# One level of Strassen's algorithm in the second MLP's first product, for the last twelve token tiles of an attention and two-MLP kernel

## The chip, the cores and the metric

The kernel runs on one core of a Trainium2 chip. The core has five engines with a queue of instructions each: PE (TensorE) multiplies matrices, DVE (VectorE), ACT (ScalarE) and POOL (GpSimd) work on elements, and SP (SyncE) issues most of the DMAs. Instructions on one engine run in the order in which they stand; an instruction that waits holds up all behind it on that engine. PE reads from SBUF and writes into PSUM, which has eight banks of 512 columns. A weight load (PEld in the profile) puts a 128x128 block into the array, and a matmul then streams up to 512 columns past it.

The metric is the time of one execution on the device in microseconds (us), as the median of several runs.

## The reference

Four batches of eight heads with 576 positions and head size 64 go through causal attention with a bias; the result, 2304 tokens of 512 values, goes through two MLPs. The change lies in the second one:

```python
def _moe2_ref(x, w_in, w_out):          # x: 2304 x 512, w_in: 512 x 2048, w_out: 2048 x 512
    h = x @ w_in
    relu6 = np.clip(h + 3.0, 0.0, 6.0)
    g = h * relu6 / 6.0
    return (g @ w_out).astype(np.float32)
```

The weights come as float64 and have to keep more than one float32r word of precision. So every operand of a product is held as two float32r parts, a high and a low one, and every product is three passes: high by high, low by high, high by low.

## The kernel before

The kernel is written as a list of steps. `plan.add` (lines 56 to 92) takes an engine, an estimated duration, a function that issues the instructions, and what the step reads and writes. `Plan.emit` (lines 94 to 165) plays the list through with these estimates: each engine takes, among the steps that are ready, the one that was added first; a step that opens a PSUM bank waits until one of the eight is free. The order so found on each engine is the program. At run time engines wait for each other by semaphores, and the order on an engine is fixed.

The second MLP (from line 1009 on) works on 18 token tiles of 128, in five chunks of 3, 3, 4, 4 and 4 tiles (`CHUNKS`). The hidden size 2048 is cut into 16 blocks `m` of 128.

- `load_w2(m)` loads one block of both weights as float64 words, decodes it and splits it into high and low (`split64`: two ACT, three DVE and one POOL or DVE step for each 128x512 tile).
- `load_x2(ci)` loads a chunk's input, which the first MLP left transposed in DRAM (`x2_d`), and splits it.
- `ffn2_h(ci, m)` is the first product: four blocks of the 512 inputs by three passes are 12 matmuls of the chunk's width (384 or 512 columns) into one bank (line 1075). Then four steps make the second product's operand: ACT takes relu(h + 3) out of the bank (L1079), DVE takes the minimum with 6 and multiplies by h (L1083), ACT rounds that to its high part (L1087), DVE subtracts to get the low part (L1091).
- `ffn2_out(ci, m, t)` is the second product: for each token tile, three matmuls of 512 columns (line 1106) add onto a bank that the tile keeps until block 15. Then ACT moves it out (L1111) and SP stores it.

Chunks 0 and 1 run interleaved, so that they share the arriving weights; their six tiles hold six banks, and two banks are left for the first products. Chunks 2, 3 and 4 run one after the other, each with four banks held and four free. The second products of a block stand two blocks (`LAG = 2`) behind its first product:

```python
    for ci, m in items:
        ...
        ffn2_h(ci, m)
        ...
        late.append((ci, m))
        if len(late) > LAG:
            outs(*late.pop(0))
```

Of the kernel before, what the change touches and what calls it, by code (L numbers as in the profile page):

```python
# [188 lines left out]
def kernel(ctx, tc, q, k, v, s, w_in, w_out, g_ln, w2_in, w2_out, out):  # L189
# [820 lines left out]
    chunks = []  # L1010
    t0 = 0
    for n in CHUNKS:
        chunks.append((t0, n))
        t0 += n
    pools, w2, xc, g_t, ob_t = {}, {}, {}, {}, {}
# [12 lines left out]
    def load_w2(m):
        def part(x, i):
            if m not in w2:  # L1030
                w2[m] = pools["w2a" if m < EARLY else "w2b"].tile([P, 2, 2, 512], F32R, name=f"w2_{m}")
# [165 lines left out]
```

## Time and profile before

| | us |
|---|---|
| median of 3 runs (lowest, highest) | 840.14 (839.83, 841.47) |
| the profiled execution | 840.16 |
| its span, first to last instruction | 838.4 |
| chunks 0 and 1 interleaved, PE only on the second MLP | about 444 to 573 |
| chunks 2, 3 and 4 | 573.2 to 834.3 |

Stages do not overlap on PE after 444 us: what PE does from there is the second MLP alone. Busy times count from an instruction's start to its modelled end, and matmuls are pipelined, so that the next one starts before the last one's end; how long a matmul holds PE is read from the distance between two starts. The granted clock is 0.995 of full speed over the span and 1.00 in every stretch of the second MLP but the last.

### The profile page before, as it was taken

The page shows a single profiled execution, that of the slowest core. Times are in us where ns is not written, and L with a number is a line of the kernel's source. Part 1 is how long each engine was busy: PE and PEld are TensorE (multiplying, and loading weights), DVE is VectorE, ACT ScalarE, POOL GpSimd, SP SyncE. Part 2 cuts the span into 40 slices and gives each one's busy share as a digit, 9 for nine tenths or more (in the row PEclk, how much of TensorE's full clock was granted, in tenths as well). Part 3 has the DMA queues.
Part 4 walks back from the last instruction along what each step waited for, and adds up shares of the span by engine and source line. Part 5 has one row for each costly group of instructions (what it writes and reads, how often), then busy time and mean ns, then how long its engine had stood idle before and what let it go on. Part 6 is the DMA issues. An engine that isn't in the chain of part 4 may idle for free.

```text
span 838.4 us, 13540 instructions
## 1 busy us (share of the span) xinstructions
PE 811.5 (97%) x4864; PEld 686.6 (82%) x4864; DVE 437.7 (52%) x1126; ACT 399.1 (48%) x928; POOL 208.2 (25%) x308
## 2 busy tenths in 40 slices
PE   3899999999999999999999999999999999999998
PEld 2555588898898889888999999998888888888886
DVE  3677887746846675739826992233222232222221
ACT  2575767755765565736635762244222322232222
POOL 1563654424632354326412220000000000000000
PEclk9999999999999999999999999999999999999999
DMA  6753596756546455223615640012000300010001
GB/s 156 198 153 109 119 225 142 173 121 134 129 112 141 102 129 121 65 93 118 199 38 191 217 151 1 0 63 89 1 0 1 101 1 0 1 51 1 0 1 50
DMA packets 95938, 77.52 MB, mean 92 GB/s; under 512 B 64288, under 2 KB 78112, under 8 KB 95872
## 3 DMA queue, kind: packets, MB, share of 16 engines
q1 hardware_dynamic: 93568, 68.27, 32.0%
q10 hardware_dynamic: 2304, 8.39, 2.9%
q8 instruction: 38, 0.62, 0.3%
q14 instruction: 28, 0.23, 0.1%
HBM read 45.38 MB, written 10.03 MB: 66 GB/s over the span
## 4 chain that ended last, share of the span: by engine, by line
PE 92%; DVE 3%; DMA 2%; POOL 1%; issue 1%; ACT 0%; SPq 0%; POOLq 0%; DVEq 0%; ACTq 0%
PE bank L1075 24%; PE bank L1106 24%; PE bank L903 11%; PE bank L816 11%; PE bank L711 6%; PE bank L614 5%; PE bank L682 5%; PE bank L587 3%; PE bank L882 2%; PE bank L477 1%; DMA rows_d<-neg 1%; DMA whole<-rows_d 1%; POOL y L630 0%; DVE y L535 0%; DMA stack<-rows_d 0%
## 5 line engine op out<-in xcount | busy, mean ns | idle before, releaser
L1075 PE MATMUL bank<-x2h,w 128*128 128x512 f32 (+1 forms) x640 | 183.9, 368 | 0.0
L1106 PE MATMUL bank<-w,gh 128*128 128x512 f32 x576 | 177.1, 390 | 0.0
L1083 DVE SCALAR_TENSOR_TENSOR g<-g,bank 128x512 f32<-128x512 f32 (+1 forms) x80 | 50.7, 633 | 204.3 <-ACT g L1079 204.0
L1075 PEld LDWEIGHTS bank<-x2h,w 128*128 128x128 f32 x640 | 118.8, 188 | 17.6
L1079 ACT ACTIVATE g<-bank 128x512 f32<-128x512 f32 (+1 forms) x80 | 44.4, 556 | 179.1 <-PE bank L1075 178.7
L1106 PEld LDWEIGHTS bank<-w,gh 128*128 128x128 f32 x576 | 107.7, 188 | 21.1
L1075 PE MATMUL bank<-x2l,w 128*128 128x512 f32 (+1 forms) x320 | 117.8, 368 | 0.0
L1106 PE MATMUL bank<-w,gl 128*128 128x512 f32 x288 | 111.8, 391 | 0.0
L535 DVE CUSTOM_DVE_ANT_0 y<-bank,mask 96x288 f32<-96x288 f32 (+4 forms) x168 | 74.7, 467 | 57.3 <-PE bank L614 38.0
L547 ACT ACTIVATE y<-y,nmax 128x256 f32<-128x256 f32 (+4 forms) x140 | 83.5, 598 | 40.9 <-DVE nmax L535 28.3
L630 POOL TENSOR_SCALAR y<-y,rsum 128x128 f32<-128x128 f32 (+4 forms) x120 | 68.5, 589 | 103.4 <-DVE rsum L626 42.8
L903 PE MATMUL bank<-zh,w_out_h 128*128 128x256 f32 x288 | 82.8, 288 | 0.0
L903 PE MATMUL bank<-zl,w_out_h 128*128 128x256 f32 x288 | 81.0, 281 | 0.0
L903 PE MATMUL bank<-zh,w_out_l 128*128 128x256 f32 x288 | 80.9, 281 | 0.0
L1091 DVE TENSOR_TENSOR gl<-g,gh 128x512 fp32r<-128x512 f32 (+1 forms) x80 | 51.8, 647 | 42.1 <-ACT gh L1087 41.8
L1087 ACT CAST gh<-g 128x512 fp32r<-128x512 f32 (+1 forms) x80 | 46.2, 578 | 47.4 <-DVE g L1083 47.3
L1075 PEld LDWEIGHTS bank<-x2l,w 128*128 128x128 f32 x320 | 60.1, 188 | 7.4
L1106 PEld LDWEIGHTS bank<-w,gl 128*128 128x128 f32 x288 | 54.0, 188 | 11.2
L816 PE MATMUL bank<-w_in_h,xh 128*128 128x512 f32 x144 | 61.2, 425 | 0.8 <-DVE xh L798 0.8
L614 PE MATMUL bank<-stack 128*96 128x288 f32 (+4 forms) x288 | 57.7, 317 | 0.5 <-DMA stack<-rows_d 0.5
L816 PE MATMUL bank<-w_in_h,xl 128*128 128x512 f32 x144 | 57.5, 399 | 0.6 <-POOL xl L802 0.6
L816 PE MATMUL bank<-w_in_l,xh 128*128 128x512 f32 x144 | 57.0, 396 | 0.0
(220 smaller groups left out, 1353.5 us busy)
## 6 DMA issues: line engine op xcount, KB each, us to landing
raw_w2i<-in_moe_w_in_dram SPq DMA_DIRECT2D x16, 512.0 KB
raw_w2o<-in_moe_w_out_dram SPq DMA_DIRECT2D x16, 512.0 KB
rawq<-in_q_dram SPq DMA_DIRECT2D x32, 144.0 KB
rawk<-in_k_dram SPq DMA_DIRECT2D x32, 144.0 KB
x_d<-x2s SPq DMA_DIRECT2D x36, 128.0 KB
out_dram<-ob SPq DMA_DIRECT2D x18, 256.0 KB
raw_wi<-in_moe_w_in_dram ACTq DMA_DIRECT2D x8, 512.0 KB
raw_wo<-in_moe_w_out_dram ACTq DMA_DIRECT2D x8, 512.0 KB
```

Source lines behind the costliest of these rows:

```text
L535: nc.vector.tensor_tensor_reduce(out=ys[h, t][:n, c0:c1], in0=bank(key)[:n, : c1 - c0], in1=mask[:n, 480 + n - w + c0 : 480 + n - w + c1], ...
L547: nc.scalar.activation(out=y[:n], in_=y[:n], func=AF.Exp, bias=nmax[:n, h, t : t + 1], scale=-1.0, accum_out=sums[:n, h, t : t + 1])
L614: nc.tensor.matmul(bank(key)[:n, : c1 - c0], lhsT=ss[:, 2 - 2 * m, ST[t] : w], rhs=ss[:, 3 - 2 * m, c0:c1], start=(m == 0), stop=(m == 1))
L630: nc.gpsimd.tensor_scalar(ys[h, t][:n], ys[h, t][:n], rsum[:n, h, t : t + 1], 1.0, ALU.mult, ALU.mult)
L711: nc.tensor.matmul(bank(key)[j * D : (j + 1) * D, lo - c0 : c1 - c0], lhsT=vs[v_key(p, a)][:n, jj, j, :], rhs=pts[pt_key(2 * p + j, a)][:n ...
L816: nc.tensor.matmul(bank(key), lhsT=xs[i][m // 2][:, kk, :], rhs=(w_in_l if m == 1 else w_in_h)[:, kk, f * 512 : (f + 1) * 512], start=(kk ...
L903: nc.tensor.matmul(bank(key)[:, : 2 * P], lhsT=w_out_at(w, kk)[:, m * P : (m + 1) * P], rhs=z[:, kk, :], start=(kk == 0 and i == 0), stop= ...
L1075: nc.tensor.matmul(bank(key)[:, :w], lhsT=wt[:, a, 0, c * P : (c + 1) * P], rhs=x[:, c, :w], start=(c == 0 and i == 0), stop=(c == KDM - 1 ...
L1083: nc.vector.scalar_tensor_tensor(out=gg, in0=gg, scalar=6.0, in1=bank(key)[:, :w], op0=ALU.min, op1=ALU.mult)
L1087: nc.scalar.copy(gh[:, :w], gg[:, :w])
L1091: nc.vector.tensor_sub(gl[:, :w], gg[:, :w], gh[:, :w].bitcast(F32))
L1106: nc.tensor.matmul(bank(key), lhsT=g_t[ci, m][1 + i // 2][:, t * P : (t + 1) * P], rhs=w2[m][:, i % 2, 1, :], start=(m == 0 and i == 0), s ...
```

## The change

The first product of tiles 6 to 17 is done by Strassen's algorithm, one level. The twelve tiles are two groups of six (768 tokens); the sixteen blocks are eight pairs `k`. For one group and one pair, the output is 256 by 768 and the sum runs over 512 inputs; each of these three is halved. Instead of eight products of halves there are seven, of sums and differences of the halves: each is two blocks of inputs by three passes, six matmuls of 384 columns.

- The weights' four sums for each pair are made from the decoded weights while chunks 0 and 1 run, on POOL for pairs 0 to 3 and on DVE for pairs 4 to 7, are split into high and low, and are stored with the three plain blocks in DRAM (`ws_d`, 1.835 MB a pair). A group loads a pair's seven forms back, two pairs at a time in SBUF.
- The input's seven forms (`xb`) are made for a group from four loads, with four subtractions on POOL and seven splits on ACT and DVE; they take the room of the input weights.
- A product's bank is not read by the gate any more: it is added on DVE (the first one copied by ACT) to sums in SBUF, from which the gate reads. So each pair and group has seven such additions on DVE and one copy on ACT.
- Chunks 0 and 1 keep their way of working. `FIRST`, `LAG` and `DELAY` stay.

The diff, cut to what the steps below touch:

```diff
-CHUNKS = (3, 3, 4, 4, 4)
+TRIO = 3
+SUMS_BEHIND = 3
+SUMS_DVE = 4
-X2_AT = 8
+X2_AT = 3
...
+    W = TRIO * P
+    ws_d = dram.tile([KFF2 // 2, P, 7, 2, 2 * P], F32, name="ws_d")
...
+    def pair_pools():
+        tops_ctx.close()
+        for name, bufs in (("ws", 2), ("mid", 1)):
+            pools[name] = ctx.enter_context(tc.tile_pool(name=name, bufs=bufs, side="right"))
...
+    def pair_parts(k):
...
+        for x in range(2):
+            plan.add("SP", 0.5, lambda x=x: store(x), reads=w2i_keys(2 * k), writes=[f"{key}/{x}"], lag=5.0, after=[f"wsd{k // 2 + 2}/3"])
...
+    def pair_sums(k):
+        T = {}
+        eng, name, us = (nc.gpsimd, "POOL", pool_tt) if k < SUMS_DVE else (nc.vector, "DVE", dve)
+        def full():
+            T["full"] = pools["sb"].tile([P, 2, 512], F32, tag="full", name=f"full{k}")
+            eng.tensor_add(T["full"], w2p[k][:, 0].bitcast(F32), w2p[k][:, 1].bitcast(F32))
+        def sums():
...
+            eng.tensor_add(sm[:, 0], a21, a22)
+            eng.tensor_sub(sm[:, 1], sm[:, 0], a11)
+            eng.tensor_sub(sm[:, 2], a11, a21)
+            eng.tensor_sub(sm[:, 3], a12, sm[:, 1])
...
+        plan.add("ACT", act(1024), high, reads=[sk], writes=[f])
+        plan.add("SP", 0.5, lambda: store_sums(0, "h"), reads=[f], writes=[f"{key}/3"], lag=5.0)
+        plan.add("DVE", dve(1024), low, reads=[f], writes=[sk])
+        plan.add("SP", 0.5, lambda: store_sums(1, "s"), reads=[sk], writes=[f"{key}/4"], lag=5.0)
...
+    def load_x2_pair(bi):
...
+        def split(i, op, room):
+            name = f"xb{bi}_{op}"
+            def high():
+                xb[bi, op] = pools[home_of(2 * room)].tile([P, 2, 2, W], F32R, tag=f"wp{room}", name=name)
+                nc.scalar.copy(xb[bi, op][:, 0], raw_x[bi, i])
...
+        def less(to, a, b):
+            plan.add("POOL", pool_tt(2 * W), lambda: nc.gpsimd.tensor_sub(raw_x[bi, to], raw_x[bi, a], raw_x[bi, b]), reads=[key(a), key(b)], writes=[key(to)])
...
+    def load_pair(bi, k):
...
+            ws[bi, k] = pools["ws"].tile([P, 7, 2, 2 * P], F32R, tag="ws", name=key)
+            nc.sync.dma_start(out=ws[bi, k].bitcast(F32), in_=ws_d[k])
+        plan.add("SP", 1.0, load, reads=["pairs", *(f"wsd{k}/{x}" for x in range(5))], writes=[key], new=[("ws", 2, key)], lag=9.0)
...
+    def pair_h(bi, k):
...
+            def mm():
+                for kc in range(2):
+                    for i, (x, y) in enumerate(((0, 0), (1, 0), (0, 1))):
+                        nc.tensor.matmul(bank(key)[:, :W], lhsT=ws[bi, k][:, WOP[op], x, kc * P : (kc + 1) * P], rhs=xb[bi, op][:, y, kc, :],
+                                         start=(kc == 0 and i == 0), stop=(kc == 1 and i == 2))
...
+            def add():
+                if to != name:
+                    g_t[to_key] = pools["mid"].tile([P, W], F32, tag=to, name=to_key)
+                if name:
+                    nc.vector.tensor_add(g_t[to_key], g_t[from_key], bank(key)[:, :W])
+                else:
+                    nc.scalar.copy(g_t[to_key], bank(key)[:, :W])
...
+        product(0)
+        sum_of("c12", "", 0)
+        product(1)
+        sum_of("c11", "c12", 1)
+        product(2)
+        sum_of("c12", "c12", 2)
+        product(5)
+        sum_of("c21", "c12", 5)
+        gate(0, "c11")
+        product(4)
+        sum_of("c12", "c12", 4)
+        sum_of("c22", "c21", 4)
+        product(3)
+        sum_of("c21", "c21", 3)
+        gate(1, "c21")
+        product(6)
+        sum_of("c12", "c12", 6)
+        gate(2, "c12")
+        gate(3, "c22")
...
+    for bi in range(2):
+        for k in range(KFF2 // 2):
+            n = bi * KFF2 // 2 + k + 2
+            if n < KFF2:
+                load_pair(*divmod(n, KFF2 // 2))
+            if (bi, k) == (0, X2_AT):
+                load_x2_pair(1)
+            pair_h(bi, k)
+            for f in todo:
+                f()
+            todo = pair_outs(bi, k)
```

Three places in the order of instructions, which are the same up to the second MLP on every engine.

PE in the steady state of the last chunk, before: one block's second products for three tiles, then the first half of the next first product. `w_10` is a weight block, `gh` and `gl` the high and low operand, `x2h` and `x2l` the input.

```order
L1106 MATMUL bank_91<-w_10_5533,gh_10_7644 128x512 x2
L1106 MATMUL bank_91<-w_10_5533,gl_10_7645 128x512
L1106 MATMUL bank_95<-w_10_5533,gh_10_7644 128x512 x2
L1106 MATMUL bank_95<-w_10_5533,gl_10_7645 128x512
L1106 MATMUL bank_92<-w_10_5533,gh_10_7644 128x512 x2
L1106 MATMUL bank_92<-w_10_5533,gl_10_7645 128x512
L1075 MATMUL bank_94<-x2h_6869,w_13_5688 128x512 x2
L1075 MATMUL bank_94<-x2l_6870,w_13_5688 128x512
L1075 MATMUL bank_94<-x2h_6869,w_13_5688 128x512 x2
L1075 MATMUL bank_94<-x2l_6870,w_13_5688 128x512
L1075 MATMUL bank_94<-x2h_6869,w_13_5688 128x512 x2
L1075 MATMUL bank_94<-x2l_6870,w_13_5688 128x512
```

One bank serves the whole first product, 12 matmuls, and four banks take turns.

PE in the steady state of a pair after the change: products 0, 1, 2, 5, 4, 3 of pair 4, then the second products of pair 3, with product 6 put among them. `xb` is a form of the input, `ws` the loaded weights, `gb` an operand of the second product, `w2o` an output weight block.

```order
L1272 MATMUL bank_96<-xb_0_6272,ws_4_6706 128x384 x6
L1272 MATMUL bank_91<-xb_1_6280,ws_4_6706 128x384 x6
L1272 MATMUL bank_96<-xb_2_6348,ws_4_6706 128x384 x6
L1272 MATMUL bank_91<-xb_5_6327,ws_4_6706 128x384 x6
L1272 MATMUL bank_96<-xb_4_6308,ws_4_6706 128x384 x6
L1272 MATMUL bank_91<-xb_3_6368,ws_4_6706 128x384 x6
L1132 MATMUL bank_95<-w2o_5358,gb_3_0_6794 128x512 x3
L1132 MATMUL bank_95<-w2o_5421,gb_3_1_6827 128x512 x2
L1272 MATMUL bank_96<-xb_6_6299,ws_4_6706 128x384 x6
L1132 MATMUL bank_95<-w2o_5421,gb_3_1_6827 128x512
L1132 MATMUL bank_93<-w2o_5358,gb_3_0_6794 128x512 x3
L1132 MATMUL bank_93<-w2o_5421,gb_3_1_6827 128x512 x3
```

The six tiles keep six banks, so seven products take turns on two banks, 96 and 91: each product goes into the bank that the product before the last one left.

DVE in such a pair, after the change: `c_4` are the sums in SBUF (line 1285 adds a bank to one), line 1100 is the gate's multiplication and line 1107 the low part. Before, DVE had lines 1083 and 1091 in turn, two instructions for 12 first-product matmuls.

```order
L1285 TENSOR_TENSOR c_4_6890<-c_4_6882,bank_91 128x384
L1285 TENSOR_TENSOR c_4_6882<-c_4_6882,bank_96 128x384
L1100 SCALAR_TENSOR_TENSOR ggb_4_0_6892<-ggb_4_0_6892,c_4_6890 128x384
L1285 TENSOR_TENSOR c_4_6908<-c_4_6882,bank_91 128x384
L1107 TENSOR_TENSOR gb_4_0_6910<-ggb_4_0_6892,gb_4_0_6910 128x384
L1285 TENSOR_TENSOR c_4_6882<-c_4_6882,bank_96 128x384
L1285 TENSOR_TENSOR c_4_6922<-c_4_6908,bank_96 128x384
L1285 TENSOR_TENSOR c_4_6908<-c_4_6908,bank_91 128x384
L1100 SCALAR_TENSOR_TENSOR ggb_4_1_6934<-ggb_4_1_6934,c_4_6908 128x384
L1285 TENSOR_TENSOR c_4_6882<-c_4_6882,bank_96 128x384
L1107 TENSOR_TENSOR gb_4_1_6943<-ggb_4_1_6934,gb_4_1_6943 128x384
L1100 SCALAR_TENSOR_TENSOR ggb_4_2_6946<-ggb_4_2_6946,c_4_6882 128x384
```

The additions that empty the two banks stand in one queue with the gate's steps of the same pair.

DVE where chunks 0 and 1 end, before: the gate's multiplication and the low part of chunk 1's blocks 12 to 15, then of chunk 2's first block.

```order
L1083 SCALAR_TENSOR_TENSOR g_12_6171<-g_12_6171,bank_97 128x384
L1091 TENSOR_TENSOR gl_12_6173<-g_12_6171,gh_12_6172 128x384
L1083 SCALAR_TENSOR_TENSOR g_13_6193<-g_13_6193,bank_94 128x384
L1091 TENSOR_TENSOR gl_13_6195<-g_13_6193,gh_13_6194 128x384
L1083 SCALAR_TENSOR_TENSOR g_14_6221<-g_14_6221,bank_92 128x384
L1091 TENSOR_TENSOR gl_14_6223<-g_14_6221,gh_14_6222 128x384
L1083 SCALAR_TENSOR_TENSOR g_15_6249<-g_15_6249,bank_98 128x384
L1091 TENSOR_TENSOR gl_15_6251<-g_15_6249,gh_15_6250 128x384
L1083 SCALAR_TENSOR_TENSOR g_0_6302<-g_0_6302,bank_97 128x512
L1091 TENSOR_TENSOR gl_0_6304<-g_0_6302,gh_0_6303 128x512
```

The same place after the change: `gs_12` to `gs_14` are the same low parts, and line 1215 makes the low parts of the first group's input forms `xb`.

```order
L1107 TENSOR_TENSOR gs_15_6256<-ggs_15_6229,gs_15_6256 128x384
L1100 SCALAR_TENSOR_TENSOR ggs_12_6260<-ggs_12_6260,bank_97 128x384
L1215 TENSOR_TENSOR xb_0_6272<-xs_0_6212,xb_0_6272 128x768
L1215 TENSOR_TENSOR xb_1_6280<-xs_1_6217,xb_1_6280 128x768
L1100 SCALAR_TENSOR_TENSOR ggs_13_6296<-ggs_13_6296,bank_94 128x384
L1215 TENSOR_TENSOR xb_6_6299<-xs_3_6254,xb_6_6299 128x768
L1215 TENSOR_TENSOR xb_4_6308<-xs_0_6212,xb_4_6308 128x768
L1215 TENSOR_TENSOR xb_5_6327<-xs_2_6234,xb_5_6327 128x768
L1107 TENSOR_TENSOR gs_12_6334<-ggs_12_6260,gs_12_6334 128x384
L1107 TENSOR_TENSOR gs_13_6340<-ggs_13_6296,gs_13_6340 128x384
L1215 TENSOR_TENSOR xb_2_6348<-xs_3_6254,xb_2_6348 128x768
L1100 SCALAR_TENSOR_TENSOR ggs_14_6363<-ggs_14_6363,bank_97 128x384
```

The low parts of blocks 12 and 13, which second products on PE wait for, now stand behind five splits of input forms. The last of these, `xb_5`, needs the third and the fourth input load and the second subtraction on POOL. On SP the fourth input load stands behind the store of the last sums' low parts (line 1184, after line 1181 on DVE), and the load of the first pair's forms (line 1248) behind both.

## Rows read from the trace of the kernel before

**Rows 1.** The page: busy time by engine, share of the chain, one weight-load group.

```profile
PE 811.5 (97%) x4864; PEld 686.6 (82%) x4864; DVE 437.7 (52%) x1126; ACT 399.1 (48%) x928; POOL 208.2 (25%) x308
...
PE 92%; DVE 3%; DMA 2%; POOL 1%; issue 1%; ACT 0%; SPq 0%; POOLq 0%; DVEq 0%; ACTq 0%
...
L1075 PEld LDWEIGHTS bank<-x2h,w 128*128 128x128 f32 x640 | 118.8, 188 | 17.6
```

**Rows 2.** Busy time by stretch: span, PE, PEld, DVE, ACT, POOL, PEclk, DMA share, GB/s.

```profile
510.00:550.00 40.00, 40.00 (x203) 36.34 (x202) 10.58 (x19) 9.43 (x19) 0.00 (x0) 1.00 0.00 1
573.20:834.30 261.10, 261.10 (x1153) 215.98 (x1151) 71.08 (x104) 70.01 (x116) 0.00 (x0) 1.00 0.06 21
450.00:460.00 10.00, 10.00 (x51) 8.90 (x50) 9.19 (x14) 7.74 (x16) 4.20 (x3) 1.00 0.86 283
```

**Rows 3.** The chain in order of time: start, us, engine and line, matmuls.

```profile
736.51 2.72 PE bank L1075 x12
739.23 8.16 PE bank L1106 x36
```

**Rows 4.** Timeline of PE, 384-column stretch: start, us, line, tiles, shape, count.

```profile
523.13 0.51 PE L1075 MATMUL bank<-x2h,w 128*128 128x384 f32 x2
...
524.72 0.51 PE L1075 MATMUL bank<-x2h,w 128*128 128x384 f32 x2
...
525.24 0.63 PE L1106 MATMUL bank<-w,gh 128*128 128x512 f32 x2
...
527.32 0.33 PE L1075 MATMUL bank<-x2h,w 128*128 128x384 f32 x1
```

**Rows 5.** Timeline of PE where chunk 1 ends and chunk 2 begins.

```profile
548.25 0.51 PE L1075 MATMUL bank<-x2h,w 128*128 128x384 f32 x2
...
566.99 0.63 PE L1106 MATMUL bank<-w,gh 128*128 128x512 f32 x2
...
569.07 0.61 PE L1106 MATMUL bank<-w,gh 128*128 128x512 f32 x2
...
573.15 0.61 PE L1075 MATMUL bank<-x2h,w 128*128 128x512 f32 x2
```

**Rows 6.** Groups of DVE, ACT, POOL by form: count, busy, mean ns of one.

```profile
L1091 DVE TENSOR_TENSOR gl<-g,gh 128x384 fp32r<-128x384 f32 x32 | 18.5, 579 | 11.5 <-ACT gh L1087 11.5
L1083 DVE SCALAR_TENSOR_TENSOR g<-g,bank 128x384 f32<-128x384 f32 x32 | 17.7, 552 | 46.5 <-ACT g L1079 46.3
L1087 ACT CAST gh<-g 128x384 fp32r<-128x384 f32 x32 | 16.4, 511 | 13.5 <-DVE g L1083 13.3
L1079 ACT ACTIVATE g<-bank 128x384 f32<-128x384 f32 x32 | 15.7, 490 | 37.2 <-PE bank L1075 37.0
L802 POOL TENSOR_TENSOR xl<-x,xh 128x512 fp32r<-128x512 f32 x16 | 21.7, 1354 | 21.2 <-DVE xh L798 18.2 <-DVE rsum L643 3.0
```

**Rows 7.** Timeline of all engines, one product handed on; brackets: idle, releaser.

```profile
520.88 0.33 PE L1075 MATMUL bank<-x2l,w 128*128 128x384 f32 x1
...
521.31 0.49 ACT L1079 ACTIVATE g<-bank 128x384 f32<-128x384 f32 x1 [2.56 <-PE bank L1075]
...
521.84 0.56 DVE L1083 SCALAR_TENSOR_TENSOR g<-g,bank 128x384 f32<-128x384 f32 x1 [2.49 <-ACT g L1079]
...
522.43 0.51 ACT L1087 CAST gh<-g 128x384 fp32r<-128x384 f32 x1 [0.62 <-DVE g L1083]
```

**Rows 8.** Timeline early in the span: PE released by DVE.

```profile
53.78 0.43 DVE L798 CAST xh<-x 128x512 fp32r<-128x512 f32 x1
...
54.26 0.50 PE L816 MATMUL bank<-w_in_h,xh 128*128 128x512 f32 x1 [0.79 <-DVE xh L798]
```

**Rows 9.** Timeline of DVE near the end of chunk 0.

```profile
548.09 0.56 DVE L1091 TENSOR_TENSOR gl<-g,gh 128x384 fp32r<-128x384 f32 x1 [0.58 <-ACT gh L1087]
```

**Rows 10.** Timelines of SP and ACT at the end: the last four output tiles.

```profile
831.01 4.46 SPq L1115 DMA_DIRECT2D out_dram<-ob  x4
...
833.16 0.60 ACT L1111 ACTIVATE ob<-bank 128x512 f32<-128x512 f32 x1 [0.81 <-PE bank L1106]
```

**Rows 11.** Timelines of POOL and of DVE at one moment.

```profile
484.65 1.49 POOL L351 TENSOR_TENSOR w<-a_w2o,w 128x512 fp32r<-128x512 f32 x1 [3.74 <-ACT w L344]
...
485.12 1.56 DVE L351 TENSOR_TENSOR w<-a_w2i,w 128x512 fp32r<-128x512 f32 x1
```

More of the change, by code (lines that the diff above doesn't have):

```diff
@@ L1009 @@
     plan.stage = "mlp2"
[L1010 to L1015, printed above, removed]
+    W = TRIO * P
+    pools, w2o, w2p, xk, g_t, ob_t = {}, {}, {}, {}, {}, {}
+    ws_d = dram.tile([KFF2 // 2, P, 7, 2, 2 * P], F32, name="ws_d")
+    tops_ctx = ExitStack()
     def first_pools():
@@ L1032, in part @@
-            return w2[m][:, x, i, :]
+            if i == 0:
+                return w2p[k][:, x, m % 2, :]
+            if m not in w2o:
+                w2o[m] = pools[home_of(m)].tile([P, 2, 512], F32R, tag=f"w2o{m}", name=f"w2o{m}")
+            return w2o[m][:, x, :]
+        home = "first" if m < EARLY else "last"
         r = []
+        if m % 2 == 0:
+            r.append(lambda: plan.add("ACT", 0.0, alloc, reads=[home], writes=[f"wp{k}/"], new=[(f"wp{k}", 1, f"wp{k}")]))
         for i, (name, src) in enumerate((("i", w2_in[:, m * P : (m + 1) * P].rearrange("(c p) f -> p c f", p=P)), ("o", w2_out[m * P : (m + 1) * P, :]))):
@@ L1093, in ffn2_h @@
-        for c in range(KDM):
-            plan.add("PE", 3 * pe(w) + 0.01, lambda c=c: mm(c), reads=[f"x2c{ci}/{x}{c}" for x in "hl"] + [f"w2i{m}/{x}w2i{m}" for x in "hl"], writes=[key],
-                     new=[("g", 2, g_key), ("gs", 3, f"gs{ci}_{m}")] if c == 0 else [], bank=key if c == 0 else None)
-        plan.add("ACT", act(w), relu, reads=[key], writes=[g_key])
-        plan.add("DVE", dve(w), times, reads=[key], writes=[g_key])
-        plan.add("ACT", act(w), high, reads=[g_key], writes=[f"gs{ci}_{m}/h"])
@@ L1099, in ffn2_h @@
-        plan.add("DVE", dve(w), low, reads=[g_key, f"gs{ci}_{m}/h"], writes=[f"gs{ci}_{m}/l"])
-    def ffn2_out(ci, m, t):
-        key = f"acc{ci}_{t}"
+            x = xk[ci, c]
+            for i, (a, b) in enumerate(((0, 0), (1, 0), (0, 1))):
+                nc.tensor.matmul(bank(key)[:, :W], lhsT=w2p[m // 2][:, a, m % 2, c * P : (c + 1) * P], rhs=x[:, b, :],
+                                 start=(c == 0 and i == 0), stop=(c == KDM - 1 and i == 2))
+        for c in range(KDM):
+            plan.add("PE", 3 * pe(W) + 0.01, lambda c=c: mm(c), reads=[f"xk{ci}{c}/{x}" for x in "hl"] + w2i_keys(m), writes=[key], bank=key if c == 0 else None)
```

201 lines of the change are left out of this document (141 added, 60 removed).

## The prediction

> **What bounds the kernel now.** I read the page first: PE is busy for 97% of the span, and the chain of work that ended last lies on PE for 92% [rows 1]. The share is an average, so the stage the change touches comes next. The busy times by stretch show PE busy for 261.10 of 261.10 us in chunks 2 to 4, at the full granted clock, with DVE and ACT near 27% and DMA at 21 GB/s [rows 2]. There PE waits for nothing; only its own instructions set the time. The chain in order of time then gives their price: a block of four tiles is 12 first-product matmuls in 2.72 us, and the 36 second-product ones of the next entry, three blocks of them, take 8.16: 226.7 ns each [rows 3]. Three chunks by 16 blocks by 24 matmuls by 226.7 ns are 261.1 us, which is the stretch. The profiled execution took 840.16 us, its span 838.4 and 1.76 around it; the median is 840.14, so the sum may be made against this execution.
>
> **Removed and added on PE.** The 12 tiles lose 576 first-product matmuls of 512 columns: 576 x 226.7 ns = 130.6 us. They gain 2 groups x 8 pairs x 7 products x 6 = 672 matmuls of 384 columns. Chunks 0 and 1 already run this shape with changing weights: from 523.13 to 525.24 there are 12 in 2.11 us, 175.8 ns each [rows 4]. The last three of them take 0.52 us, 173.3 ns, which is the best price. At 175.8 the products cost 118.1 us.
>
> The 576 second products stay, but not at one price. After a change from 384 to 512 columns nine of them take 2.08 us, 231.1 ns each (525.24 to 527.32 [rows 4]); of 27 in a row the first nine take 2.08 us and the next 18 take 4.08, 226.7 each [rows 5]. In a pair product 6 stands among the second products, so they are entered twice, with 5 and with 31. I price 14 at 231.1 and 22 at 226.7: 8.22 us. A pair is then 42 x 0.1758 + 8.22 = 15.61 us, and 16 pairs are 249.7 against 261.1: 11.4 us less. With every second product at 231.1 it is 9.8 less, with 173.3 and 226.7 throughout 14.1 less.
>
> A page gives another sum, which I don't use. By the Trainium skill ("TensorE: Matmul & The Clock Gate", section "Back-to-back issue gap") a matmul of N columns costs N/2.4 ns plus about 2.5, by my estimate 162.5 and 215.8 ns. Products for first-product matmuls would then bring 124.3 - 109.2 = 15.1 us. The trace has 175.8 and 226.7 [rows 3, 4], and 12.5 by the same subtraction.
>
> **Handing back two banks.** Six tiles keep six banks, so seven products rotate on two: before product n+2 starts, the addition of product n has to be done. A product is six matmuls, 1.05 us, so this must happen within 2.1 us of its start. Nowhere before does a bank come back that fast, so I build it from steps. A product's last matmul starts 0.88 after the first, lasts 0.33 as recorded, and the reader starts 0.10 later [rows 7]: 1.31. The addition reads a bank as line 1083 does, 0.55 [rows 6]: 1.86. DVE to PE is 0.05 [rows 8]: 1.91. That leaves 0.2 us at each place, if DVE is free. It is busy with about 15 instructions of 0.55 to 0.58 in 15.6 us; behind one of the gate's multiplications (line 1100 stands between two additions) an addition starts some 0.1 late. Product 4 is read by two additions, but the next product on its bank stands five second products later, 1.15 us of cover. The hops come from single rows, so I take 0.1 us a pair, 1.6 us. The ends are 0 and, if each of four reuses in a pair stalls by 0.3, 19 us.
>
> **Making and storing the weight sums.** In chunks 0 and 1 this adds some 24 us to DVE (twelve instructions of 1024 columns at 1.5 us and sixteen of 256 at 0.39, estimated from the 384-column rows [rows 6] by width), with eight conversions on ACT and work on POOL. Until about 500 us DVE is nearly full, 9.19 of 10 [rows 2], because it decodes weights; later it has 10.58 of 40. The sums of pairs 4 to 7 fall into that later part; second products stand two blocks behind the first product, over 8 us of cover. Taken: 0; if the cover is gone, one late low part costs its own 0.6 to 1.2 us.
>
> **The transition.** As many matmuls stand ahead of product 0 as before up to 569.07 [rows 5], since 18 second products of chunk 1 now come after the first pair. The input loads wait until chunk 0's last first product (548.25 [rows 5] and 2.11 us more) has freed their room. Pair 7's sums start on DVE after chunk 0's block 14, at 548.65 [rows 9], and end with the low parts near 554.6 (1.5 + 1.5 + 1.5 us on DVE and 1.4 on ACT between, scaled by width from [rows 6]). SP stores them there, then issues the fourth input load and the first pair's weights. At 283 GB/s [rows 2] and 2 us for landing [rows 10], 2.6 MB of inputs and sums are there near 560 and 1.8 MB of weights near 567, ahead of 569. But `xb_5` needs the fourth load, then the second subtraction on POOL (768 columns: 1354 x 1.5 = 2.0 us [rows 6]), a conversion on ACT (1.0) and one on DVE (1.2): 564 to 565. The low part of block 12 stands behind it, and its second products would start at 562.8, going back from 569.07 by 18 x 0.2311 and 12 x 0.1758 [rows 4]. That is about 2 us late. Next is `xb_3`, three products' time behind; and the second group's `xb_0`, which waits for a load behind 3.7 MB of weights, stands on DVE ahead of the first additions (bank reuse by product 6): another 0 to 2 us. Together I take 2.5; ends 0 and 13, the latter if the loads run at half that rate.
>
> POOL's four subtractions there run beside DVE's splits. By the Trainium skill ("SBUF — State Buffer", section "Who interferes with whom") a GpSimd read fully blocks a DVE instruction with two SBUF inputs. Here a 512-column DVE subtraction beside one on POOL took 1.56 us [rows 11], against 0.77 if the 384-column one's 579 ns [rows 6] is scaled. By that rule a split could wait out a whole subtraction, 2.0 us; if that fell on `xb_5` the term would be 4.5 and the sum 835.4. The row shows about 0.8 us of delay, so I leave 2.5.
>
> **Other places.** In a pair 1.835 MB of weights take 6.5 us at 283 GB/s, twice 15.6 is there to load them: 0. The second group's inputs are split in pairs 3 to 7, among the additions: 0.5 (0 to 2). At the end the same tile is last. Output buffers come back within 2.1 us, since the copy at 833.16 waited only for PE and its buffer's store was issued at 831.01 [rows 10]: 0.
>
> **Sum.** 840.16 - 11.4 + 1.6 + 2.5 + 0.5 = 833.4 us.
>
> **Rivals.** The first ends slower: the two-bank rotation stalls. If a bank comes back about 0.33 us later than the 1.91 I built, PE waits at four places in each of 16 pairs. The point of no change is 11.4 - 3.0 = 8.4 us over 64 places, 0.13 each. At 0.3 us it is 19.2: 840.16 - 11.4 + 3.0 + 19.2 = 851.0. For it: DVE has one queue for additions and gate, and every hop is short of cover. Against it: the steps, each measured, leave 0.2. Chance 0.12.
>
> The second: the transition is late by 8 to 13 us, because loads, stores and 3.7 MB of weights share one queue at less than 283 GB/s: 839 to 844, middle 841. For it: SP issues in order and waits for the last sums. Against it: 283 GB/s was seen with two streams of loads [rows 2]. Chance 0.12.
>
> The third: 384-column matmuls go at the pace of their weight loads, recorded as 188 ns each [rows 1]. 672 x 0.188 + 131.6 = 257.9, 3.2 less than before, and with 4.6 of costs 841.6. For it: PEld was busy for 36.34 of 40 us in that stretch [rows 2]. Against it: 175.8 ns were measured there. Chance 0.04.
>
> That the change doesn't do what it says is out: the order has 672 matmuls where 576 stood.
>
> **How the numbers follow.** The forecast has 0.70, the rivals 0.12, 0.12 and 0.04, and 0.02 is left for what I don't see. Its own range is 828 to 838: 14.1 gained and 2 lost, or 9.8 gained and 7.5 lost. A measurement here can tell 0.2%, 1.7 us, from no change. The second and third rivals lie around 840, half of them inside those 1.7 us or close by, a quarter faster. Faster: 0.69 + 0.05 = 0.74; same 0.09; slower 0.12 + 0.05 = 0.17. The range reaches to 841.
>
> **What would show it.** Right: 672 matmuls at a pace near 176 ns; 15.6 to 15.8 us from pair to pair; PE without waits for DVE inside a pair; a gap of about 2 us near 563; a span near 831.6. Wrong: an idle PE ahead of line 1272 in every pair, released by line 1285 (first rival); a gap over 6 us between 560 and 585 (second); 188 ns from start to start (third).

## The result and the profile after

The change makes the kernel slower: 844.65 us as the median of five runs (843.66 to 845.88) against 840.14, a ratio of 1.0052 with a 95% interval of 1.0037 to 1.0066. The forecast was 833.4, with 828 to 838 as its own range and 841 as the outer end, so the time lies outside it and on the other side of no change. The profiled execution took 844.44 us, 4.28 more than that of before; its span is 842.6, 4.2 more.

From the page of the kernel after: busy time by engine, the chain's share by engine, and the group of the new products (before: [rows 1]).

```profile
PE 805.1 (96%) x4960; PEld 698.2 (83%) x4960; DVE 544.1 (65%) x1300; ACT 422.6 (50%) x986; POOL 254.6 (30%) x336
...
PE 80%; DVE 11%; DMA 4%; issue 2%; POOL 2%; ACT 1%; SPq 0%; DVEq 0%; POOLq 0%; ACTq 0%
...
L1272 PE MATMUL bank<-xb,ws 128*128 128x384 f32 x672 | 122.7, 336 | 0.6 <-DVE c L1285 0.6
```

PE has less to do than before, 805.1 us against 811.5, and yet the chain is on PE for only 80% instead of 92%, with 11% on DVE. Time was saved on PE and lost in waiting for DVE.

Where? The timeline of PE after, at its gaps and at the pairs (start, us, line, tiles, shape, count, idle before and its releaser); a row of many matmuls stands for one unbroken run (before: [rows 4, 5]).

```profile
456.30 0.62 PE L1120 MATMUL bank<-xk,wp 128*128 128x384 f32 x2 [1.50 <-ACT xk L1079]
457.41 1.43 PE L1120 MATMUL bank<-xk,wp 128*128 128x384 f32 x4 [0.49 <-DVE xk L1083]
...
499.26 2.38 PE L1120 MATMUL bank<-xk,wp 128*128 128x384 f32 x12 [0.96 <-DVE ggs L1100]
...
505.12 2.35 PE L1120 MATMUL bank<-xk,wp 128*128 128x384 f32 x12 [1.16 <-DVE ggs L1100]
...
515.21 2.35 PE L1120 MATMUL bank<-xk,wp 128*128 128x384 f32 x12 [1.47 <-DVE ggs L1100]
...
518.33 1.89 PE L1132 MATMUL bank<-w2o,gs 128*128 128x512 f32 x7 [0.30 <-DVE gs L1107]
...
520.82 2.35 PE L1120 MATMUL bank<-xk,wp 128*128 128x384 f32 x12 [0.61 <-DVE ggs L1100]
...
558.65 4.35 PE L1120 MATMUL bank<-xk,wp 128*128 128x384 f32 x24
...
577.17 3.36 PE L1132 MATMUL bank<-w2o,gs 128*128 128x512 f32 x7 [3.30 <-DVE gs L1107]
...
584.63 7.47 PE L1272 MATMUL bank<-xb,ws 128*128 128x384 f32 x42
591.94 4.28 PE L1132 MATMUL bank<-w2o,gs 128*128 128x512 f32 x18
596.06 7.47 PE L1272 MATMUL bank<-xb,ws 128*128 128x384 f32 x42
...
611.57 6.44 PE L1272 MATMUL bank<-xb,ws 128*128 128x384 f32 x36
...
627.13 6.44 PE L1272 MATMUL bank<-xb,ws 128*128 128x384 f32 x36
```

Chunk 0's last first product starts at 558.65; before, it started at 548.25 [rows 5], 10.4 us earlier. The seven gaps up to 521 hold 6.5 of these; the rest is a lower clock behind the first two (the granted clock from 459 to 461 is 0.50) and what the modelled ends of the matmuls ahead of a gap hide. Product 0 starts at 584.63, 15.56 after the 569.07 of before [rows 5], so another 5.2 went between the two. From there to the end it is 842.6 - 584.63 = 257.97 us, where before needed 838.4 - 569.07 = 269.33: 11.36 saved. The difference, 15.56 - 11.36, is the 4.2 us of the span. From pair to pair it is 627.13 - 611.57 = 15.56 us; 15.61 was forecast.

The busy times of both kernels in the stretch in which chunks 0 and 1 decode their weights: stretch, its length, PE, PEld, DVE, ACT, POOL, PEclk, DMA share, GB/s. First before, then after.

```profile
445.00:523.00 78.00, 78.00 (x392) 70.57 (x391) 57.76 (x96) 45.87 (x88) 16.77 (x12) 1.00 0.46 149
```

```profile
445.00:523.00 78.00, 71.51 (x343) 62.38 (x342) 73.76 (x91) 46.23 (x85) 44.17 (x32) 0.98 0.62 202
```

DVE goes from 57.76 to 73.76 of 78 us, full but for the start, and POOL from 16.77 to 44.17. PE, which was busy without a break, loses 6.5 us there, and its granted clock is 0.98: behind the gaps at 456 it ran at 1.2 GHz, half its clock, for a while. What filled DVE is read from its groups by form (count, busy, mean ns). Before, 444 to 540:

```profile
L1091 DVE TENSOR_TENSOR gl<-g,gh 128x384 fp32r<-128x384 f32 x23 | 13.5, 587 | 6.2 <-ACT gh L1087 6.2
...
L351 DVE TENSOR_TENSOR w<-a_w2i,w 128x512 fp32r<-128x512 f32 x12 | 9.0, 767 | 0.1
...
L331 DVE TENSOR_SCALAR t_w2i<-raw_w2i 128x512 int32<-128x512 uint32 x10 | 4.6, 460 | 0.0
```

After, 444 to 523:

```profile
L1107 DVE TENSOR_TENSOR gs<-ggs,gs 128x384 fp32r<-128x384 f32 x15 | 15.3, 1021 | 0.6 <-ACT gs L1104 0.6
L353 DVE TENSOR_TENSOR wp<-a_w2i,wp 128x512 fp32r<-128x512 f32 x12 | 14.3, 1197 | 0.0
...
L1100 DVE SCALAR_TENSOR_TENSOR ggs<-ggs,bank 128x384 f32<-128x384 f32 x15 | 8.1, 543 | 6.1 <-ACT ggs L1097 6.1
L333 DVE TENSOR_SCALAR t_w2i<-raw_w2i 128x512 int32<-128x512 uint32 x10 | 8.1, 810 | 0.0
...
L1181 DVE TENSOR_TENSOR s<-s,full 128x1024 fp32r<-128x1024 f32 x3 | 3.6, 1213 | 0.0
```

These are the same instructions on the same shapes: the gate's low part (L1091, now L1107), the weights' low part (L351, now L353), the decode's unit step (L331, now L333). They take 1021 instead of 587 ns, 1197 instead of 767, 810 instead of 460. The gate's multiplication, which has one operand in PSUM, takes what it took (543, before 552 [rows 6]). By count times difference of the means, these groups and the smaller ones beside them (the decode's other steps and the low parts of the input) add 17.5 us to DVE; its new instructions up to 523, the low parts of three pairs' sums (L1181), are 3.6.

Taken one by one, the records say what stretched them. Of the 15 low parts of the gate, the eight without a POOL instruction beside them take 541 to 551 ns, the seven with one 1087 to 2737. The multiplications take 538 to 555 either way. One moment shows it, in the timelines of POOL and of DVE after:

```profile
447.69 2.40 POOL L1166 TENSOR_TENSOR full<-wp 128x1024 f32<-128x1024 f32 x1 [23.53 <-DVE ggs L1100]
...
447.77 2.74 DVE L1107 TENSOR_TENSOR gs<-ggs,gs 128x384 fp32r<-128x384 f32 x1 [0.58 <-ACT gs L1104]
```

DVE's low part takes 2.74 us instead of 0.56 and ends 0.4 after POOL's addition: it waited for POOL's whole instruction and then did its own work. The Trainium skill ("SBUF — State Buffer", section "Who interferes with whom") says that the ports which DVE and GpSimd share are an exclusive lock, and that a DVE instruction with at most one input in SBUF, outside its two-port modes, does not contend. The 2.74 us and the unchanged 543 ns agree. The unit step has one input in SBUF too and was stretched all the same: without POOL beside it 411 to 421 ns, beside POOL up to 2626. By that section this needs a two-port mode of it. That it takes 416 ns where the low part of as many columns takes 680 fits such a mode, and no run here shows it directly.

The transition in the chain of waits of the kernel after (start, us, what):

```profile
562.76 6.08 DMA xs<-x_d
...
572.46 2.58 DVE xb L1215
575.04 2.08 DVE gs L1107
```

And DVE and POOL there, from their timelines:

```profile
569.78 5.26 DVE L1215 TENSOR_TENSOR xb<-xs,xb 128x768 fp32r<-128x768 f32 x3 [1.49 <-ACT xb L1212]
574.97 2.62 DVE L1107 TENSOR_TENSOR gs<-ggs,gs 128x384 fp32r<-128x384 f32 x2
577.51 0.95 DVE L1215 TENSOR_TENSOR xb<-xs,xb 128x768 fp32r<-128x768 f32 x1
...
571.84 4.87 POOL L1218 TENSOR_TENSOR xs<-xs,xs 128x768 f32<-128x768 f32 x2 [0.99 <-DVE xb L1215]
```

The fourth input load issues at 562.76 and lands 6.1 us later; behind it come ACT's and DVE's splits up to `xb_5`, which is done at 575.04, with the last of the three at 2.58 us, and then block 12's low part, which takes 2.08 us beside POOL's fourth subtraction. Without POOL beside them a split takes 0.95 us (the one at 577.51) and a low part 0.55, so these two hold 3.16 us of stretch. PE waits 3.3 us for the low part, so another order on DVE or a silent POOL would each close most of the gap. PE then runs slowly, as the busy times of two stretches show (stretch, its length, PE, PEclk, DMA share, GB/s):

```profile
577.00:579.00 2.00, 1.83 (x4) 0.54 0.87 237
579.00:581.00 2.00, 2.00 (x8) 0.61 0.94 358
```

PE came back at 1.2 GHz, half its clock. The seven second products from 577.17 to 580.33 take 3.16 us; at 231.1 ns each [rows 4] they would take 1.62, so the clock cost 1.5 us.

### The profile page after: what moved, and what is told of

The parts are those of the page before. It is cut to its first block, busy times and chain, and to the rows that moved or that the text cites. A ratio compares the mean times of both kernels' runs of the same rounds, so it can differ in the third digit from the quotient of the medians.

```text
span 842.6 us, 14160 instructions
## 1 busy us (share of the span) xinstructions
PE 805.1 (96%) x4960; PEld 698.2 (83%) x4960; DVE 544.1 (65%) x1300; ACT 422.6 (50%) x986; POOL 254.6 (30%) x336
## 4 chain that ended last, share of the span: by engine, by line
PE 80%; DVE 11%; DMA 4%; issue 2%; POOL 2%; ACT 1%; SPq 0%; DVEq 0%; POOLq 0%; ACTq 0%
PE bank L1132 19%; PE bank L1272 14%; PE bank L905 11%; PE bank L818 10%; PE bank L713 6%; PE bank L616 5%; PE bank L684 5%; PE bank L1120 4%; PE bank L589 3%; PE bank L884 2%; DVE gs L1107 2%; DVE wp L353 2%; PE bank L479 1%; DVE t_w2i L333 1%; DVE a_w2o L337 1%
## 5 line engine op out<-in xcount | busy, mean ns | idle before, releaser
L1132 PE MATMUL bank<-w2o,gb 128*128 128x512 f32 x576 | 136.4, 391 | 0.0
L1132 PEld LDWEIGHTS bank<-w2o,gb 128*128 128x128 f32 x576 | 107.7, 188 | 21.0
L1272 PE MATMUL bank<-xb,ws 128*128 128x384 f32 x672 | 122.7, 336 | 0.6 <-DVE c L1285 0.6
L1272 PEld LDWEIGHTS bank<-xb,ws 128*128 128x128 f32 x672 | 118.3, 188 | 3.5 <-DVE c L1285 1.0
L1285 DVE TENSOR_TENSOR c<-c,bank 128x384 f32<-128x384 f32 x112 | 60.3, 552 | 83.7 <-PE bank L1272 70.0
L1120 PE MATMUL bank<-xk,wp 128*128 128x384 f32 x384 | 74.8, 343 | 6.2 <-DVE ggs L1100 4.2
L1132 PE MATMUL bank<-w2o,gs 128*128 128x512 f32 x288 | 74.4, 403 | 3.6 <-DVE gs L1107 3.6
L1120 PEld LDWEIGHTS bank<-xk,wp 128*128 128x128 f32 x384 | 68.6, 191 | 11.1 <-DVE ggs L1100 6.2
L1132 PEld LDWEIGHTS bank<-w2o,gs 128*128 128x128 f32 x288 | 54.8, 193 | 14.7 <-DVE gs L1107 4.9
L905 PEld LDWEIGHTS bank<-zh,w_out_h 128*128 128x128 f32 x288 | 54.3, 189 | 1.1 <-DVE zl L891 0.2
```

Source lines behind the costliest of these rows:

```text
L905: nc.tensor.matmul(bank(key)[:, : 2 * P], lhsT=w_out_at(w, kk)[:, m * P : (m + 1) * P], rhs=z[:, kk, :], start=(kk == 0 and i == 0), stop= ...
L1120: nc.tensor.matmul(bank(key)[:, :W], lhsT=w2p[m // 2][:, a, m % 2, c * P : (c + 1) * P], rhs=x[:, b, :], start=(c == 0 and i == 0), stop=( ...
L1132: nc.tensor.matmul(bank(key), lhsT=g_t[name][:, i // 2, (t % TRIO) * P : (t % TRIO + 1) * P], rhs=w2o[m][:, i % 2, :], start=(m == 0 and i ...
L1272: nc.tensor.matmul(bank(key)[:, :W], lhsT=ws[bi, k][:, WOP[op], x, kc * P : (kc + 1) * P], rhs=xb[bi, op][:, y, kc, :], start=(kc == 0 and ...
L1285: nc.vector.tensor_add(g_t[to_key], g_t[from_key], bank(key)[:, :W])
```

## The experiments

Theory A: POOL's sums stretch what DVE does beside them, DVE is full until 521, and PE waits. B: DVE's own added instructions fill it. C: the added stores delay the arriving weights. D: the 5 us at the transition are the order on DVE. E: the way of the inputs through DRAM sets them. Each run is compared by its ratio to the kernel before on the same chip (median of before 840.5 to 840.6).

**POOL's sums left out**

```diff
 def full():   # and sums(), for pairs 0 to 3
-    eng.tensor_add(T["full"], w2p[k][:, 0].bitcast(F32), w2p[k][:, 1].bitcast(F32))
...
-    eng.tensor_add(sm[:, 0], a21, a22)
...
-nc.scalar.copy(T["h"].bitcast(F32R), T["s"])
+nc.scalar.copy(T["h"].bitcast(F32R), T["from"])   # a plain block
```

> Left out: the additions and subtractions on POOL that make the weight sums of pairs 0 to 3 (20 instructions, 26.7 us of POOL); their split on ACT and DVE reads a plain weight block of the same size instead, and all stores and loads stay. Theory A (POOL's reads beside DVE stretch DVE's instructions, so that DVE is full until 521 instead of 503 and PE waits for it): the mean of the gate's low part in 444 to 540 falls from 905 to about 590 ns, the decode's low part from 1197 to about 770, PE's gaps before 523 go, and product 0 starts 8 to 10 us earlier: 834.5 to 837 us. Theory B (DVE's own added instructions, the low parts of the sums, fill it): 843 to 845. Theory C (the added stores delay the arriving weights): 843 to 845.

835.17 us, ratio 0.9941 (0.9918 to 0.9963). The busy times in the decode, two of DVE's groups from 444 to 523, and PE at the transition:

```profile
445.00:523.00 78.00, 77.91 (x393) 70.33 (x392) 66.21 (x103) 49.27 (x92) 17.66 (x12) 1.00 0.72 236
```

```profile
L1107 DVE TENSOR_TENSOR gs<-ggs,gs 128x384 fp32r<-128x384 f32 x17 | 11.5, 678 | 1.2 <-ACT gs L1104 1.2
...
L353 DVE TENSOR_TENSOR wp<-a_w2i,wp 128x512 fp32r<-128x512 f32 x12 | 8.1, 684 | 1.1 <-ACT wp L346 1.1
```

```profile
568.37 2.67 PE L1132 MATMUL bank<-w2o,gs 128*128 128x512 f32 x7 [3.47 <-DVE gs L1107]
...
575.83 7.47 PE L1278 MATMUL bank<-xb,ws 128*128 128x384 f32 x42
```

No gap before 523, DVE at 66.2 us, its low parts back from 1021 to 678 ns and from 1197 to 684, product 0 8.8 us earlier. POOL still has the decode's own low parts, and some of the gate's low parts beside those are still long (up to 1648 ns). DVE's low parts of the sums and all stores are still there (the DMA share is 0.72, in the change 0.62), so B and C are out for the decode, and A holds. The gap at the transition is about the same, 3.47 us: POOL's four subtractions there were left in.

**All sums on DVE**

```diff
-SUMS_DVE = 4
+SUMS_DVE = 0
```

> The sums of pairs 0 to 3 on DVE too (five instructions, about 2.9 us a pair), nothing on POOL but the decode's low parts. Theory A: DVE's instructions go back to their lengths of before (17 us less in 444 to 523), against 9 to 12 us more of its own: 840 to 843 us. Theory B: 9 to 12 us more of DVE's work come on top: 850 to 856.

844.59 us, 1.0043 (1.0025 to 1.0061).

```profile
445.00:523.00 78.00, 77.78 (x389) 69.77 (x388) 68.62 (x113) 48.11 (x88) 17.46 (x11) 1.00 0.64 203
```

```profile
521.61 1.88 PE L1132 MATMUL bank<-w2o,gs 128*128 128x512 f32 x7 [0.22 <-DVE gs L1107]
...
570.44 2.93 PE L1132 MATMUL bank<-w2o,gs 128*128 128x512 f32 x6 [6.10 <-ACT gs L1104]
```

The decode came out by A: 13.8 us more of DVE's own work and only 0.22 us of gaps, with DVE at 68.6 us in place of 73.8. The total was missed, because the last sums now fall into the transition, beside POOL's subtractions and ahead of the splits, and PE waits 6.1 us there. ACT also stands 9.8 us at the copy of an output tile, of which more below.

**DVE's low parts left out**

```diff
-        plan.add("DVE", dve(1024), low, reads=[f], writes=[sk])
+        if k >= SUMS_DVE:
+            plan.add("DVE", dve(1024), low, reads=[f], writes=[sk])
```

> Left out: DVE's low part of the weight sums of pairs 0 to 3 (four instructions of 1.2 us, three of them before 521; the store takes the sums themselves). POOL's work stays. Theory A: at most 3 x 1.2 us and what POOL stretches beside them, 1 to 4 us less: 840.5 to 843.5. Theory B: most of the 10 us: 834 to 837.

847.69 us, 1.0095 (1.0079 to 1.0111): against B, which wanted 834 to 837, and outside A's numbers too. With the low parts gone the planner puts POOL's sums sooner (the second pair's at 464.9 instead of 475.4), beside other steps of the decode; the low parts of gate and weights are shorter (871 and 901 ns) and another step of the decode, L337, takes 1428 ns instead of 1129. DVE is busy for 72.46 of the 78 us, nearly as before the edit. The gaps moved (1.83 us at 485, 1.74 at 508), and why it is slower than the change itself was not followed further.

**The input's steps behind the last gates in the list**

```diff
-            load_x2_pair(0)
...
+    load_x2_pair(0)      # after the loop over chunks 0 and 1
```

> The steps that load and split the first group's input come later in the list than the last first products of chunk 1 with their gates, so the low parts of blocks 12 to 15 stand ahead of the input's splits on DVE wherever both are ready. Theory D (the 5 us lost at the transition are that order: 3.3 us of waiting and 1.5 us of a halved clock behind it): product 0 starts 3 to 5 us earlier, 839.5 to 842 us. Theory E (the loads of the input and of the first weights set product 0): no change, 844 to 845, with the gap now ahead of product 0.

843.78 us, 1.0045 (1.003 to 1.0061). The order on DVE at the place stayed as it was, since the planner took the splits to be ready first; the gap stayed too, 3.32 us. It tells nothing on D. But behind this gap the granted clock stayed at 1.00 (577 to 581), and product 0 came 0.9 us sooner than in the change.

**The loads' estimate at 9 us**

```diff
-new=[(f"xk0{i}", 1, key(i))], lag=4.0)
+new=[(f"xk0{i}", 1, key(i))], lag=9.0)
```

> One number: the planner's estimate of how long the input loads take to land, 4 us, becomes 9 (6 to 9 were traced). The low parts of blocks 12 and 13 of chunk 1 then stand behind two of the input's splits on DVE instead of five; the sums on POOL stay. Theory D (the 5 us at the transition are that order): the gap of 3.3 us ahead of block 12's second products goes, and so does the halved clock behind it: product 0 starts 3 to 5 us earlier, 839.5 to 841.5 us. Theory E (the loads set product 0): no gain, the gap moves to product 0 or product 3, 843.5 to 845.

851.21 us, 1.013 (1.0116 to 1.0143). The gap at 573 went, as D says, and a worse one came, which neither theory had. The chain, ACT and PE in that run:

```profile
569.79 12.16 DMA out_dram<-obacc
...
582.06 0.60 ACT L1137 ACTIVATE obacc<-bank 128x512 f32<-128x512 f32 x1 [9.52 <-DMA out_dram<-obacc]
...
587.82 1.01 PE L1272 MATMUL bank<-xb,ws 128*128 128x384 f32 x2 [5.12 <-ACT xb L1212]
590.72 7.86 PE L1272 MATMUL bank<-xb,ws 128*128 128x384 f32 x28 [1.90 <-DVE xb L1215]
```

ACT stood 9.5 us at the copy of chunk 0's third output tile. Its buffer comes free when an earlier tile's store has landed, and that store stood on SP's queue behind two loads of 1.8 MB; it landed 12.16 us after its issue. The input's splits stood behind the copy on ACT. Call this F. In the change itself ACT waits 6.76 us at the same copy, but product 0 starts there without a gap.

**Output stores on ACT's queue, with the 9 us**

```diff
-            nc.sync.dma_start(out=out[r0 : r0 + P, :], in_=ob_t.pop(key))
+            nc.scalar.dma_start(out=out[r0 : r0 + P, :], in_=ob_t.pop(key))
...
-            plan.add("SP", 0.5, store, reads=[f"ob{key}"], writes=[f"out{key}"], lag=2.0)
+            plan.add("ACT", 0.1, store, reads=[f"ob{key}"], writes=[f"out{key}"], lag=3.0)
```

> The run with the 9 us estimate (851.2 us) and one more edit: the output tiles' stores are issued by ACT into its own DMA queue instead of by SP behind 3.7 MB of weight loads. Theory F (in that run ACT stood 9.5 us at the copy of chunk 0's third tile, whose buffer came free only when a store behind the weight loads had landed, and the input's splits stood behind it): the gaps of 5.1 and 1.9 us inside the first pair go, product 0 at 580 to 582, 839.5 to 842.5 us. Theory E (the way through DRAM itself sets the inputs): still 848 to 851.

842.48 us, 1.0022 (1.0013 to 1.0032): 8.7 us less than without the edit, inside F's numbers and outside E's.

```profile
570.21 0.35 ACTq L1141 DMA_DIRECT2D out_dram<-obacc  x1
...
579.98 0.60 ACT L1137 ACTIVATE obacc<-bank 128x512 f32<-128x512 f32 x1 [4.05 <-DMA out_dram<-obacc]
...
585.19 5.14 PE L1272 MATMUL bank<-xb,ws 128*128 128x384 f32 x28 [1.09 <-DVE xb L1215]
```

The gap of 5.12 is gone and that of 1.90 is 1.09; ACT's wait for the store fell from 9.52 to 4.05 us with the same loads under way. Two things are in this, and the run does not part them. The store came back sooner: issued at 570.21, it had landed when the copy began at 579.98, 9.8 us later at most, instead of 12.16. And ACT's order changed: the planner, which got other estimates for the store, put two of the input's splits (573.45 and 575.09) ahead of the third copy, which stood behind it before. By the chain, the wait at that copy was what held the inputs; how much of the 8.7 us the queue brought, and how much the order, stays open.

The Trainium skill ("DMA: Bandwidth & Descriptors", section "Queues, rings and completion order") has each DMA engine take turns between queues, packet by packet. The packet records agree: on ACT's queue the store's packets of 2 KB run from 574.2 to 579.1, among the loads' packets of 14 KB, which run to 580.7; on SP's queue, in the run before, they start at 579.7, when the last of the loads' packets leave (580.4).

Against the change itself (1.0052) the two edits bring about 0.3%; POOL's subtractions are still there, and 0.68 us of gap is left ahead of block 12's second products.

**A slower hand-back of the banks**

```diff
                 if name:
+                    px = g_t[from_key][:, :PROBE]        # 384 columns
+                    nc.vector.tensor_copy(px, px)
                     nc.vector.tensor_add(g_t[to_key], g_t[from_key], bank(key)[:, :W])
```

> Each of the seven additions that empty a bank gets one more DVE instruction in front of it, a copy of its 384-column sum in SBUF onto itself (some 0.3 us by the 0.43 us of a 512-column conversion). The trace of the change shows the additions done 0.25 to 0.3 us before the product that reuses the bank. If that margin is all there is: 0.05 to 0.3 us of waiting at some four places in 16 pairs, 850 to 862 us. If the two-bank rotation has more room than that: 844 to 847.

852.86 us, 1.0148 (1.0133 to 1.0164). DVE's copies and PE at two pairs in a row:

```profile
L1287 DVE COPY c<-c 128x384 f32<-128x384 f32 x35 | 12.5, 356 | 17.1 <-ACT c L1290 16.8
```

```profile
743.95 6.70 PE L1273 MATMUL bank<-xb,ws 128*128 128x384 f32 x36
...
759.80 6.69 PE L1273 MATMUL bank<-xb,ws 128*128 128x384 f32 x36
```

Each copy takes 0.356 us, seven a pair, and the pair grows from 15.56 to 15.85 us: 0.29, or 0.07 at each of four places, 4.6 us in 16 pairs. The rest lies outside the steady pairs (product 0 is 1.6 us later, and the gap at the groups' boundary grows from 0.65 to 2.74). So the total came out by the smaller margin, but only about half of it at the places that were meant. If a copy delays its addition by its own length, a delay of 0.36 that costs 0.07 leaves a margin of about 0.3 us at each place, which is an estimate.

**Combinations.** With the sums on DVE, the input's steps after the loop, the 9 us, and further edits:

```diff
-SUMS_DVE = 4
-SUMS_BEHIND = 3
+SUMS_DVE = 0
+SUMS_BEHIND = 1          # the first two runs; then 3, 3 and 2
...
-            plan.add("POOL", pool_tt(2 * W), lambda: nc.gpsimd.tensor_sub(raw_x
+            plan.add("DVE", dve(2 * W), lambda: nc.vector.tensor_sub(raw_x      # all but the second
...
-writes=[f"{key}/3"], lag=5.0)
+writes=[f"{key}/3"], lag=3.5)      # and "/4": the first, second and fourth
...
-writes=[f"out{key}"], lag=2.0)
+writes=[f"out{key}"], lag=9.0)      # the first two; then ACT's queue
```

> Together: all sums on DVE and two blocks sooner in the list, their stores' estimate 3.5 instead of 5 us, the input's steps behind the last gates in the list with the 9 us estimate, its subtractions on DVE instead of POOL, output stores estimated at 9 us. Theory A and D together: no gaps before 523 and 0 to 3 us at the transition, product 0 at 569 to 572.5, 829.5 to 833.5 us. If what is lost at the transition is the data's way through DRAM (theory E): 834 to 840, with a gap ahead of product 0 or product 3.

839.68 us, 0.999 (0.9977 to 1.0004): outside the numbers of A and D, inside those of E.

> As the run before, but the input's four subtractions stay on POOL (2.0 us each beside DVE's splits). Theory A: the splits beside them take about 2 us instead of 0.95 and the inputs are ready 2 to 5 us later; how much of that reaches product 3: 0 to 3 us more than the run before.

837.67 us, 0.9974 (0.9963 to 0.9985): not worse: the median is 2 us lower, and the intervals overlap. In this order, POOL's four subtractions cost no more than the same work on DVE. Both had new gaps in the decode, 3.5 and 3.8 us between 511 and 554. The chain of waits of the second shows one of the things that they waited for:

```profile
503.41 6.15 DMA raw_w2o<-in_moe_w_out_dram
```

Raw weights, landing late (and again at 514.59, 4.08 us): this is C, which came with the edits that put the sums and their stores sooner. At the third tile's copy ACT stood 4.7 us in the first run and 2.7 in the second (F).

> All sums on DVE at the same place in the list as in the change (three blocks behind), the input's steps behind the last gates with the 9 us estimate and its subtractions on DVE, output stores on ACT's queue. Theories A, D and F together: the decode as in the run with the sums on DVE (0.2 us of gaps before 523), no gap inside the first pair, product 0 at 569.5 to 573: 830 to 834 us. If something else limits the transition: a gap ahead of product 0 or 3 and 835 to 840.

833.54 us, 0.9909 (0.9896 to 0.9923). With the output stores on ACT's queue the total is below the 835 to 840 that were to mean another limit. Product 0 starts at 577.76, later than expected, because the planner put it behind all the second products of chunk 1.

> As the run before, with the planner's estimate of the sums' stores at 3.5 instead of 5 us, which puts the last sums ahead of the input's splits. 0 to 2 us either way of the run before: 829 to 835.

832.99 us, 0.9905 (0.9891 to 0.9919).

> As the first of these with the sums two blocks behind instead of three (5 us estimate). More of DVE's summing falls into the decode: 0 to 3 us of gaps before 545, the transition as good: 830 to 836.

831.85 us, 0.9887 (0.987 to 0.9904): 1.1% faster than before, the lowest median of all. The decode and the first pairs of this run:

```profile
445.00:523.00 78.00, 78.00 (x397) 70.92 (x397) 68.63 (x112) 46.44 (x86) 15.77 (x10) 1.00 0.65 207
```

```profile
576.20 7.54 PE L1272 MATMUL bank<-xb,ws 128*128 128x384 f32 x42 [0.74 <-issue]
...
584.51 7.45 PE L1272 MATMUL bank<-xb,ws 128*128 128x384 f32 x42
```

The second pair starts at 584.51, in the change at 596.06. With A, D and F taken away together the kernel is 8.7 us faster than before, most of the 11.4 that the products save; what the rest is was not followed.

## Why the prediction was wrong

**Making and storing the weight sums, taken at 0, is the step that failed.** It counted DVE's own 24 us, the eight conversions on ACT and "work on POOL", and saw cover for them. It left out what POOL's work costs DVE: 17.5 us of stretch just while DVE decodes. The row was there [rows 11]; I used it for POOL's four subtractions at the transition and not for the 20 instructions, 26.7 us, that stand beside a DVE busy for 9.19 of 10 us [rows 2]. I also read its 0.8 us as the size of such a delay. In that row DVE's instruction ends 0.54 us after POOL's: it waited for POOL's end, and a longer instruction on POOL would have cost it more. Cost: chunk 0's last first product is 10.4 us late; without POOL's part of the sums it is 1.4 us late, and the kernel takes 835.2 us.

**The transition was found but priced at half:** 2.5 against 5.2 us. The walk to `xb_5` came out at the right time: 564 to 565, with the 10.4 us of delay 574.4 to 575.4, and it was 575.04. That is partly luck: the fourth load landed at 568.8, before the 570.4 that the walk has with the delay, and the split took 2.58 us instead of 1.2. Block 12's low part then took 2.08 us beside POOL, 1.5 more than I gave it, and the halved clock behind the gap, 1.5 us, was not in the sum. The rule of the Trainium skill ("SBUF — State Buffer", section "Who interferes with whom"), by which I had the term at 4.5, came nearer than the 2.5 I kept: a split did wait out a subtraction, and it fell on `xb_5`.

**Right:** the work on PE. Products at 175.8 ns and second products at 226.7 to 231.1 made 15.61 us a pair; it is 15.56. Costs of 1.6 for the banks and 0.5 for the second group's inputs were hardly drawn on: 11.36 us were saved where 11.4 stood before costs. That output buffers come back at once (0) was read at the end, where no loads run; at chunk 0's third tile ACT waited 6.76 us, which cost PE nothing there.

**The rivals.** The first, stalls in the two-bank rotation, did not happen: ahead of the 672 products PE stood 0.65 us for an addition, once, at the groups' boundary; delaying each addition by 0.36 us brought 0.07 at a place. The third, the pace of weight loads, did not either: 42 products take 591.94 - 584.63 = 7.31 us, 174 ns each. Of the second a part came, 5.2 us, by order and POOL and not by a slow queue: product 0 started without a gap. None of them was the main cause, which lay in a term I had closed.

## What to carry to other kernels

When work goes to POOL beside a nearly full DVE, price it twice: once on POOL and once as the stretch of what DVE does meanwhile, from a moment in the trace where both already run together. A step called hidden needs the engine that hides it, and the slack of that engine after the step's side effects. A planner that is told 4 us for a load that takes 6.1 puts waiting work ahead of ready work.

## What the runs showed of the hardware

DVE's subtractions of two inputs in SBUF waited out POOL's instructions: the gate's low part took 541 to 551 ns alone and 1087 to 2737 beside POOL, while the multiplication with one operand in PSUM took 538 to 555 either way. Not every subtraction beside POOL was held: two low parts of the weight sums kept their 1.21 us.

A 256 KB store issued behind 3.7 MB of loads on the same queue landed 12.2 us after its issue; on ACT's queue, with the same loads under way, after 9.8 us at most.

The gap of 3.3 us at the transition cost nearly half as much again, since PE came back from it with a granted clock of 0.54 to 0.61. That price is not sure: behind a gap of 3.32 us in the run with the input's steps behind the last gates the clock stayed at 1.00.
